# Stage one of a Fourier transform by float32r products of split sums, and a back stage given out later

## The chip, the cores and the metric

The kernel runs on one core of a Trainium2 chip. The metric is the device time of one execution in microseconds. Five engines work side by side, each through its own instructions in order: PE (matrix products, with a weight load before each, "PEld"), DVE, ACT and POOL (elementwise work) and SP (here only transfers). They wait for each other through semaphores.

## The reference

```python
def _attn_ref(x, w_r, w_i, b_r, b_i):            # x: 8 x 3008 x 256
    X = np.fft.rfft(x, axis=1)
    Yr = Xr @ w_r - Xi @ w_i + b_r
    Yi = Xr @ w_i + Xi @ w_r + b_i
    ...                                          # both shrunk: sign(Y) * max(|Y| - 0.01, 0)
    return np.fft.irfft(Y, n=3008, axis=1).astype(np.float32)

def _moe_ref(x, w_in, w_out):                    # x: 24064 x 256, w_in: 256 x 2048
    r = np.maximum(x @ w_in, 0.0)
    return ((r * r) @ w_out).astype(np.float32)
```

The output of the first is the input of the second.

## The kernel before, in words

**The transform.** 3008 is 64 x 47. The forward transform of a batch is done in two stages. Stage one (class `Fwd`, and `Fwd2` for the second batch) works on 13 units of 120 rows: two rows of the input are added and subtracted (`fold`, POOL, line 214, tile `xs`), and each of sum and difference is multiplied by a 120x120 matrix of cosines or sines (`am32`, line 235) in float32. The result is copied by ACT to `xe` and stored to DRAM (line 224). Stage two (class `Pair`) works on 12 pairs of groups in a batch: it loads stage one's result (`ka`), multiplies (line 279), mixes with the weights (line 300), shrinks, and goes back by the inverse matrix (`back`, line 332); `store_back` stores the result split in two (`kuh`, `kul`). `Back` loads that (`du`) and does the last transform (lines 455 to 459), whose output `yr` is the input of the second part.

**Products of split numbers.** Most products are done in float32r, a shorter format of the same four bytes. A float32 number is split into a high part and the rest, `hi` by a cast on ACT (line 97) and `lo` by a subtraction on POOL or DVE (line 101; both in `halves`), and a product is the sum of three: hi x hi, lo x hi, hi x lo. Stage one is done in plain float32; in the profile each float32 product shows as two records.

**The second part.** The tokens of a batch are six tiles of 500 or 504. For each tile there are eight steps of 21 float32r products with `win` (7 sums by a scheme of Strassen's kind; tile `psh`) and 12 with `wout` (`pso`). Between them stand DVE (sums, `mc`), ACT (relu, square, and the cast to `mg`'s high part) and POOL (`mg`'s low part). The input of a tile is split into `yt` in four pieces (`Tokens.split`); the last piece is needed by the second product of the tile's first step, and POOL writes its low part.

**The order.** The main loop runs over half steps, 96 in a batch. In each it issues half of a step and the jobs due by then: a job has a due time in half steps, for a pair `start + j * step` with fixed distances (`fwd` at 0, `sums` at 1.0, `mix` at 2.1 and 3.0, `shrink` at 4.0, `back(0)` at `end`, `back(1)` 0.9 later), for a unit of stage one its load 2.5 before, its fold 0.8 before and its product 0.3 after its time. While batch b is in the second part, the pairs of b + 1 and stage one of b + 2 are done. These are priorities: a scheduler lays the final order of each engine at build time from its own estimate of the times, and the engines then follow that order. Within the second part the order of the products is fixed (`then`). `T` takes a buffer of a named pool; the number of buffers of a name is in `MAIN` (2 if it isn't listed).

## Time and profile before

| | |
|---|---|
| median of 3 runs | 2624.49 us (2619.64 to 2627.85) |
| the profiled execution | 2624.28 us, its span 2622.5 us |
| busy, share of the span | PE 98%, DVE 68%, ACT 64%, POOL 63% |
| stage one by float32 (line 235) | 312 records of 379 ns, 199.4 to 2030.3 us |
| fold (line 214) | 156 instructions, 750 ns each |
| mean granted clock of TensorE | 0.992 |

A row of the timeline gives the start in microseconds, the duration, the engine, the line, the operation, what is written and read, and how many equal instructions it stands for; in brackets how long the engine had been idle before it and for whom. Rows of the waits give the total, the number and the longest in microseconds. Products overlap on PE, so a single record is longer than the distance from one to the next.

### The profile page before, as it was taken

To read this page: it belongs to the slowest core of one execution; us is meant where nothing else is said; L and a number is where in the kernel's file an instruction comes from. 1 tells how busy PE (TensorE), PEld (TensorE's weight loads), DVE (VectorE), ACT (ScalarE), POOL (GpSimd) and SP (SyncE) were. 2 spreads that over 40 slices of the span, in tenths; PEclk is the share of its full clock that TensorE was granted. 3 is DMA by queue.
4 is the path that set the end of the run, shared out by engine and by line. 5 is a ranking of instruction groups with operands and counts; after the bars stand their busy time and mean duration, and the time that the engine had idled before them with its cause. 6 is when DMAs were issued, how large, how long until landed. Compare 5 with 4: busy or idle time off the path is not lost.

```text
span 2622.5 us, 47568 instructions
## 1 busy us (share of the span) xinstructions
PE 2568.5 (98%) x16908; PEld 2348.8 (90%) x16908; DVE 1779.7 (68%) x3797; ACT 1671.7 (64%) x2433; POOL 1654.6 (63%) x1628
## 2 busy tenths in 40 slices
PE   6799999999999999999999999999999999999999
PEld 4688989999999999999999999999999999999998
DVE  6866766676666767577675776767767677765554
ACT  3466656666666666666666666666666666666665
POOL 3246656766676667667675676666666666666564
PEclk8899999999999999999999999999999999999999
DMA  8643333233422333223332333323332223221100
GB/s 269 195 140 98 113 108 89 83 108 92 117 85 81 108 105 96 85 86 110 107 95 85 96 99 107 94 75 104 99 104 88 72 81 95 76 66 38 36 17 17
DMA packets 191455, 250.51 MB, mean 96 GB/s; under 512 B 21755, under 2 KB 135923, under 8 KB 191219
## 3 DMA queue, kind: packets, MB, share of 16 engines
q1 hardware_dynamic: 178915, 225.12, 28.3%
q0 software_dynamic: 12304, 22.35, 3.7%
q8 instruction: 136, 2.23, 0.4%
q14 instruction: 100, 0.82, 0.1%
HBM read 146.85 MB, written 100.53 MB: 94 GB/s over the span
## 4 chain that ended last, share of the span: by engine, by line
PE 91%; DVE 3%; DMA 2%; POOL 2%; issue 1%; ACT 1%; SPq 0%; POOLq 0%; ACTq 0%; DVEq 0%
PE pso L478 38%; PE psh L478 34%; PE psf L300 7%; PE psf L279 3%; PE psf L235 2%; PE psf L332 2%; PE psf L458 1%; PE psf L459 1%; PE psf L455 1%; DMA s<-xe 1%; POOL mg L101 1%; DMA du<-s 1%; PE psf L409 1%; DMA x<-x_in 0%; DVE df L151 0%
## 5 line engine op out<-in xcount | busy, mean ns | idle before, releaser
L101 POOL TENSOR_TENSOR mg<-mc,mg 128x500 fp32r<-128x500 f32 (+1 forms) x768 | 973.6, 1288 | 587.5 <-ACT mg L97 557.7
L478 PE MATMUL pso<-mg,wout 128*128 128x500 f32 (+1 forms) x4608 | 1180.6, 393 | 3.9 <-POOL mg L101 2.6
L478 PE MATMUL psh<-yt,win 128*128 128x250 f32 (+1 forms) x8064 | 1070.1, 281 | 1.4 <-POOL yt L101 1.4
L478 ACT ACTIVATE mc<-mc 128x1000 f32<-128x1000 f32 (+1 forms) x768 | 802.4, 1045 | 411.5 <-DVE mc L478 402.5
L478 PEld LDWEIGHTS psh<-yt,win 128*128 128x128 f32 x8064 | 1020.6, 189 | 33.7 <-POOL yt L101 1.6
L478 PEld LDWEIGHTS pso<-mg,wout 128*128 128x128 f32 x4608 | 819.4, 189 | 132.7 <-POOL mg L101 4.8
L478 DVE TENSOR_TENSOR mc<-psh,mv 128x500 f32<-128x500 f32 (+3 forms) x768 | 419.4, 548 | 433.8 <-PE psh L478 401.8
L97 ACT CAST mg<-mc 128x1000 fp32r<-128x1000 f32 (+1 forms) x384 | 396.9, 1034 | 18.6 <-ACT mc L478 0.7
L478 DVE TENSOR_TENSOR mv<-psh,mu 128x500 f32<-128x500 f32 (+1 forms) x384 | 260.8, 679 | 55.6 <-PE psh L478 24.2
L300 PE MATMUL psf<-wx,kxh 128*128 128x256 f32 x1008 | 207.8, 282 | 1.4 <-ACT kxh L97 0.9
L98 DVE COPY mp<-psh 128x250 f32<-128x250 f32 (+1 forms) x384 | 160.0, 417 | 35.3 <-PE psh L478 11.5
L300 PEld LDWEIGHTS psf<-wx,kxh 128*128 128x128 f32 x1008 | 167.2, 189 | 5.9 <-ACT kxh L97 1.1
L101 POOL TENSOR_TENSOR ksl<-kv,ksh 128x512 fp32r<-128x512 f32 x84 | 108.6, 1293 | 95.8 <-ACT ksh L97 95.6
L478 DVE TENSOR_TENSOR mu<-psh,mp 128x250 f32<-128x250 f32 (+1 forms) x384 | 160.7, 419 | 11.5
L214 POOL TENSOR_TENSOR xs<-xt 120x256 f32<-120x256 f32 x156 | 114.0, 750 | 85.0 <-DMA xt<-x_in 77.3
L478 DVE TENSOR_TENSOR mc<-psh,mp 128x250 f32<-128x250 f32 (+1 forms) x384 | 157.1, 409 | 4.7 <-PE psh L478 3.1
L321 DVE TENSOR_TENSOR kv<-psf,ke 64x256 f32<-64x256 f32 x336 | 141.8, 422 | 22.4 <-PE psf L300 13.7
L300 PE MATMUL psf<-wx,kxl 128*128 128x256 f32 x504 | 141.5, 281 | 0.9 <-DVE kxl L101 0.9
L97 ACT COPY dy<-psf 128x188 f32<-128x188 f32 x256 | 76.6, 313 | 88.0 <-PE psf L459 87.8
L97 ACT CAST ksh<-kv 128x512 fp32r<-128x512 f32 x84 | 52.0, 619 | 118.4 <-DVE kv L101 112.7
L312 DVE TENSOR_TENSOR ke<-psf,bias 128x512 f32<-128x512 f32 x84 | 58.1, 691 | 100.2 <-PE psf L300 100.0
L97 ACT CAST kuh<-psf 128x256 fp32r<-128x256 f32 x192 | 68.5, 373 | 85.9 <-PE psf L332 67.4
(97 smaller groups left out, 2563.6 us busy)
## 6 DMA issues: line engine op xcount, KB each, us to landing
du<-s SPq DMA_DIRECT2D x128, 256.0 KB, 2.9
s<-kuh SPq DMA_DIRECT2D x192, 128.0 KB, 1.8
s<-kul SPq DMA_DIRECT2D x192, 128.0 KB, 1.9
s<-xe SPq DMA_DIRECT2D x92, 240.0 KB, 2.4
xt<-x_in SPq DMA_DIRECT2D x91, 240.0 KB, 3.5
kcm<-cm_in POOLq DMA_DIRECT2D x84, 256.0 KB, 3.3
ka<-s SPq DMA_DIRECT2D x84, 256.0 KB, 3.5
du<-s SPq DMA_DIRECT2D x256, 64.0 KB, 2.7
```

The source lines that it names most:

```text
L97: return act.copy(out=out, in_=in_)
L98: return eng.tensor_copy(out=out, in_=in_)
L101: return eng.tensor_tensor(out=out, in0=a, in1=b, op=ALU.subtract)
L214: return eng.tensor_tensor(out=out[:, :n], in0=self.xt[:, :n, 0], in1=self.xt[:, :n, 1], op=(ALU.add, ALU.subtract)[t])
L235: nc.tensor.matmul(ps[:M1, t], am32[:, t], self.u[:, t], start=True, stop=True)
L279: nc.tensor.matmul(pv[:, :, c, g, :], self.a[:, g, c * 128:(c + 1) * 128], bg, start=True, stop=True)
L300: self.last = nc.tensor.matmul(ps, l, wx[j][:, k, c, :], start=n == 0, stop=n == 5)
L312: dve.tensor_add(out=self.e, in0=self.pe, in1=bias)
L321: dve.tensor_add(out=v[64 * r:64 * r + 64, g], in0=ps[gs], in1=self.e[gs, r])
L332: nc.tensor.matmul(ps[:, :D], self.cm[:, g, j * 128:(j + 1) * 128], r[:, g], start=n == 0, stop=n == 2)
L409: nc.tensor.matmul(ps[:, :D], self.x[:, c, js], w32[j][:, c], start=n == 0, stop=n == 3)
L478: last_of[eng] = op(*args, **kwargs)
```

## The change

Stage one of the six last batches (class `Fwd`, 78 units) is done in float32r. After the fold the sums `xs` are split into `xh` (ACT) and `xl` (POOL), which share the two buffers of `xt`; the matrices are split once into `amh` and `aml`, the latter in the buffer of `nam`, after its last reader. Each of a unit's two float32 products becomes three. `Fwd2`, the second batch, stays as it was. And `end`, the due time of a pair's back stage, goes from 7.1 to 9.1 for the pairs of all but the first batch of the main loop, where it was 9.1 already. Line numbers behind the class `Fwd` grow by three (235 is 238, 279 is 282, 300 is 303, 332 is 335, 478 is 481).

```diff
@@ class Fwd
         def add(self):
-            self.u = T("xs", [M1, 2, D], F32)
+            u = T("xs", [M1, 2, D], F32)
             for t in range(2):
-                self.fold(pool, self.u[:, t:t + 1], t)
+                self.fold(pool, u[:, t:t + 1], t)
+            self.uh = T("xh", [M1, 2, D], F32R, tag="xt")
+            self.ul = T("xl", [M1, 2, D], F32R, tag="xt")
+            halves(self.uh, self.ul, u, pool)

         def run(self):
             ps = bank([128, 2, D])
             for t in range(2):
-                nc.tensor.matmul(ps[:M1, t], am32[:, t], self.u[:, t], start=True, stop=True)
+                for n, (a, u) in enumerate(((amh, self.uh), (aml, self.uh), (amh, self.ul))):
+                    nc.tensor.matmul(ps[:M1, t], a[:, t], u[:, t], start=n == 0, stop=n == 2)
...
-    nam = T("nam", [M1, M1], F32)
-    act.mul(nam, am32[:, 1], -1.0)
+    nam = T("nam", [M1, 2, M1], F32)
+    act.mul(nam[:, 0], am32[:, 1], -1.0)
...
-                first, step, end = 1.0, 6.1, 7.1
+                first, step, end = 1.0, 6.1, 9.1
...
         if m == max(LATER):
             conv.close()
             pools.update(dict.fromkeys(CONV), **dict.fromkeys(SIDE, memory(ctx, "side")))
+            amh, aml = (T(name, [M1, 2, M1], F32R, tag=tag) for name, tag in (("amh", "amh"), ("aml", "nam")))
+            halves(amh, aml, am32, pool)
```

With the jobs the scheduler's order changes. Three places of it follow; a name ends in the number of its buffer, and `x2` stands for two rows alike.

The first is PE at the start of the third tile (`yt_2391` and `yt_2392`, in the change `yt_2411` and `yt_2412`, are its high and low parts). Before, from the tile's first product:

```order
L478 MATMUL psh_2683<-yt_2391,win_81 128x250
L478 MATMUL psh_2683<-yt_2391,win_82 128x250
L478 MATMUL psh_2683<-yt_2392,win_81 128x250
L332 MATMUL psf<-ksh,kcm 128x256 x2
L332 MATMUL psf<-ksl,kcm 128x256
L235 MATMUL psf<-xs,am_76 120x256 x2
L279 MATMUL psf<-kb,ka 128x2x64 x4
```

Then come the three products that read the last piece. In the change:

```order
L481 MATMUL psh_2715<-yt_2411,win_81 128x250
L335 MATMUL psf<-ksh,kcm 128x256 x2
L335 MATMUL psf<-ksl,kcm 128x256
L481 MATMUL psh_2715<-yt_2411,win_82 128x250
L481 MATMUL psh_2715<-yt_2412,win_81 128x250
L238 MATMUL psf<-xh,amh 120x256
L238 MATMUL psf<-xh,aml 120x256
L238 MATMUL psf<-xl,amh 120x256
```

The same three of L238 follow for the difference, then the four of L282, and then thirteen products of L303 and six of L335, which are new here, before the one that reads the low part of the last piece.

The second is POOL up to the third tile's last split. Before:

```order
L101 TENSOR_TENSOR yt_2392<-yr,yt_2391 128x500
L494 TENSOR_TENSOR ms<-yr,ms 128x250
L101 TENSOR_TENSOR mg_2558<-mc,mg_2557 128x504 x2
L101 TENSOR_TENSOR yt_2392<-ms,yt_2391 128x500
L101 TENSOR_TENSOR ms<-yr,ms 128x250
L108 DMA kcm<-cm_in 128x512
L471 COPY yr<-dy 128x2x184
L101 TENSOR_TENSOR yt_2392<-ms,yt_2391 128x500
L101 TENSOR_TENSOR ksl<-kv,ksh 128x512
L214 TENSOR_TENSOR xs<-xt 120x256 x2
L101 TENSOR_TENSOR mg_2643<-mc,mg_2642 128x504 x2
```

In the change:

```order
L101 TENSOR_TENSOR yt_2412<-yr,yt_2411 128x500
L101 TENSOR_TENSOR mg_2586<-mc,mg_2585 128x504 x2
L497 TENSOR_TENSOR ms<-yr,ms 128x250
L101 TENSOR_TENSOR yt_2412<-ms,yt_2411 128x500
L108 DMA kcm<-cm_in 128x512
L101 TENSOR_TENSOR ms<-yr,ms 128x250
L474 COPY yr<-dy 128x2x184
L101 TENSOR_TENSOR ksl<-kv,ksh 128x512
L101 TENSOR_TENSOR mg_2671<-mc,mg_2670 128x504 x2
L214 TENSOR_TENSOR xs<-xt 120x256 x2
L101 TENSOR_TENSOR yt_2412<-ms,yt_2411 128x500
```

The last split (the last row with `yt`) went behind ksl, the next mg and the next xs. An xl stands above these rows.

The third is POOL up to the fifth tile's last split. Before:

```order
L101 TENSOR_TENSOR yt_3926<-yr,yt_3925 128x500
L214 TENSOR_TENSOR xs<-xt 120x256 x2
L494 TENSOR_TENSOR ms<-yr,ms 128x250
L101 TENSOR_TENSOR yt_3926<-ms,yt_3925 128x500
L101 TENSOR_TENSOR mg_4177<-mc,mg_4176 128x500 x2
L108 DMA kcm<-cm_in 128x512
L101 TENSOR_TENSOR ms<-yr,ms 128x250
L101 TENSOR_TENSOR ksl<-kv,ksh 128x512
L101 TENSOR_TENSOR kxl<-kp,kxh 128x256
L471 COPY yr<-dy 128x2x124
L101 TENSOR_TENSOR yt_3926<-ms,yt_3925 128x500
```

In the change:

```order
L101 TENSOR_TENSOR yt_3994<-yr,yt_3993 128x500
L101 TENSOR_TENSOR yt_3994<-ms,yt_3993 128x500
L101 TENSOR_TENSOR ms<-yr,ms 128x250
L214 TENSOR_TENSOR xs<-xt 120x256 x2
L101 TENSOR_TENSOR mg_4141<-mc,mg_4140 128x500 x2
L474 COPY yr<-dy 128x2x124
L101 TENSOR_TENSOR yt_3994<-ms,yt_3993 128x500
```

Before, `mg_4177` was the 32nd step's; in the change `mg_4141` is the 31st step's. The split went ahead of the 32nd, and a kcm, a ksl and a kxl went from above it to below.

6 lines of the change are left out of this document (3 added, 3 removed).

## The prediction

> **What bounds the kernel now.** I read the page's busy shares and its chain of waits first, then the busy time of each engine by stretches of the span.
>
> ```profile
> PE 2568.5 (98%) x16908; PEld 2348.8 (90%) x16908; DVE 1779.7 (68%) x3797; ACT 1671.7 (64%) x2433; POOL 1654.6 (63%) x1628
> PE 91%; DVE 3%; DMA 2%; POOL 2%; issue 1%; ACT 1%; SPq 0%; POOLq 0%; ACTq 0%; DVEq 0%
> 300.00:500.00 200.00, 193.93 (x1267) 177.03 (x1266) 132.03 (x276) 122.36 (x179) 124.75 (x126) 0.97 0.35 100
> 500.00:800.00 300.00, 299.98 (x2018) 276.43 (x2018) 204.52 (x441) 195.99 (x285) 203.86 (x204) 1.00 0.33 96
> 1700.00:2000.00 300.00, 299.76 (x2020) 276.38 (x2019) 207.71 (x443) 195.56 (x286) 203.97 (x204) 1.00 0.33 96
> ```
>
> The columns of the last three rows are PE, PEld, DVE, ACT and POOL busy, then granted clock, DMA share and GB/s. From 500 us on PE is never without a matmul (299.98 and 299.76 of 300), at full clock, and the chain that ends last is PE for 91%. There PE work taken away is time taken away, for as long as the helpers keep delivering. They have room: POOL is busy 203.86 of 300 (68%), ACT 195.99 (65%). The exception is the first batch. Between 200 and 500 us PE loses time at two places, and both matter for the change:
>
> ```profile
> 240.00:262.00 22.00, 19.31 (x125) 17.26 (x124) 13.95 (x29) 11.44 (x19) 17.45 (x19) 1.00 0.37 107
> 350.00:384.00 34.00, 27.96 (x163) 24.68 (x162) 19.04 (x41) 16.54 (x31) 22.06 (x25) 0.85 0.45 123
> ```
>
> The first loses 22.00 - 19.31 = 2.7 us, at full clock. The second is idle 34.00 - 27.96 = 6.0 us and has a mean clock of 0.85, which costs another 0.15 x 34 = 5.1 us: 11.1 us in all. Together 13.8 us.
>
> **Stage one on PE.** A unit's two float32 products (L235) give way to six float32r products of the same 256 columns. Both prices stand side by side in the trace, with a stream of float32r products (L300, six for each of two mixes) right before a unit of stage one:
>
> ```profile
> L235 PE MATMUL psf<-xs,am 120*120 120x256 f32 x312 | 81.2, 379 | 1.3 <-DVE kv L321 1.3
> 1018.65 0.28 PE L300 MATMUL psf<-wx,kxh 128*128 128x256 f32 x1
> ...
> 1020.06 1.03 PE L235 MATMUL psf<-xs,am 120*120 120x256 f32 x4
> 1008.10 2.60 PE L478 MATMUL psh<-yt,win 128*128 128x250 f32 x21
> ```
>
> The 312 records are 78 units of four, two records to a float32 product. A row that merges several records lasts one full record plus the starts in between, so records start every (1.03 - 0.379) / 3 = 0.217 us, and a unit holds PE for 4 x 0.217 = 0.868 us. The twelve float32r products start from 1018.65 to 1020.06: 1.41 / 12 = 0.1175 us each. Six cost 0.705 us. A unit saves 0.163 us, 78 units 12.7 us. The trace has no float32r product of 120 rows. The nearest row on the cheap side is the 250-column stream, (2.60 - 0.281) / 20 = 0.116 us, where 0.281 is the 0.28 us of one record as in the L300 row: 0.172 us a unit, 13.4 us. On the dear side, the saving is gone only at 0.868 / 6 = 0.145 us a product, a quarter above any stream shown. I take 12.7, since L300 has the very width.
>
> The Trainium skill ("FP8 and Floating Point Precision", TensorE Precision Notes) says that true FP32 takes four passes through the array. By that rule three passes instead of four would save a quarter of 0.868, an estimate of 16.9 us in all; the trace agrees on four passes only roughly, since a float32r product costs 0.1175 us and not the 0.1085 us of half a record.
>
> **The added split.** Each unit gains an ACT cast and a POOL subtraction of 120x512. The rows of the nearest shape, 128x512, and POOL's waits for xt, of which the rivals speak:
>
> ```profile
> L101 POOL TENSOR_TENSOR ksl<-kv,ksh 128x512 fp32r<-128x512 f32 x84 | 108.6, 1293 | 95.8 <-ACT ksh L97 95.6
> L97 ACT CAST ksh<-kv 128x512 fp32r<-128x512 f32 x84 | 52.0, 619 | 118.4 <-DVE kv L101 112.7 <-PE psf L332 5.5
> ```
>
> ```profile
> POOL xs L214 <- DMA xt<-x_in: 77.3, 44, 6.5
> ```
>
> 78 x 1.293 = 100.9 us more on POOL, 78 x 0.619 = 48.3 us more on ACT. With 13 units in a batch of 96 half steps this raises POOL from 68% to about 73%. In steady state it is hidden by POOL's idle time. What it costs if that cover is gone shows at a tile boundary, where POOL is busiest:
>
> ```profile
> 686.59 2.49 POOL L101 TENSOR_TENSOR mg<-mc,mg 128x500 fp32r<-128x500 f32 x2
> 689.04 1.07 POOL L101 TENSOR_TENSOR yt<-ms,yt 128x500 fp32r<-128x500 f32 x1
> 691.10 0.69 PE L478 MATMUL pso<-mg,wout 128*128 128x500 f32 x2
> 693.22 2.60 PE L478 MATMUL psh<-yt,win 128*128 128x250 f32 x21
> ```
>
> The tile's last split (yt) ends at 690.1. Of the 21 products from 693.22, nine still belong to the tile before and three don't need this split, so it is wanted at 693.22 + 12 x 0.116 = 694.6: 4.5 us to spare. The first half of mg ends near 687.9 and is wanted at 691.1: 3.2 us to spare. One xl of 1.29 us ahead of them is covered, two (2.6 us) nearly use it up. The new order puts one ahead of this place, and I count 0.5 us for all such places, between 0 and 3.
>
> **The two places of the first batch.** At the third tile PE waits for the last split:
>
> ```profile
> 237.03 1.44 POOL L214 TENSOR_TENSOR xs<-xt 120x256 f32<-120x256 f32 x2 [2.79 <-DMA xt<-x_in]
> 246.69 1.10 PE L235 MATMUL psf<-xs,am 120*120 120x256 f32 x4 [1.28 <-DVE kv L321]
> 249.47 1.06 POOL L101 TENSOR_TENSOR yt<-ms,yt 128x500 fp32r<-128x500 f32 x1
> 247.63 1.06 PE L279 MATMUL psf<-kb,ka 128*128 128x128 f32 x8
> 250.58 1.08 PE L478 MATMUL psh<-yt,win 128*128 128x250 f32 x7 [1.42 <-POOL yt L101]
> 255.95 2.51 POOL L101 TENSOR_TENSOR mg<-mc,mg 128x504 fp32r<-128x504 f32 x2
> ```
>
> POOL works without a pause from 237.03 to 250.53. The new order puts four more things ahead of that split: xl (1.29), ksl (1.29), the next mg (2.51) and the next xs (1.44), 6.5 us, so the split ends near 257.1. PE for its part has most of a pair's mix and two more groups' back stages ahead of the product that needs it. Summed by the prices above, with 0.9 us for the eight records of L279, that product moves from 2.7 to 4.8 us behind the tile's first, so from 249.2 (250.58 - 1.42) to about 251. The wait grows from 1.4 to some 6 us; if the 1.28 us in front of L235 goes, the place loses 6.4 instead of 2.7: +3.7 us. Without the reordering of PE it would be +6.5.
>
> The fifth tile is the second place:
>
> ```profile
> 354.78 1.42 POOL L214 TENSOR_TENSOR xs<-xt 120x256 f32<-120x256 f32 x2 [2.49 <-DMA xt<-x_in]
> 357.45 3.50 PE L478 MATMUL pso<-mg,wout 128*128 128x500 f32 x8 [2.42 <-POOL mg L101]
> 374.71 1.07 POOL L101 TENSOR_TENSOR yt<-ms,yt 128x500 fp32r<-128x500 f32 x1
> ```
>
> ```profile
> 356.00:359.00 3.00, 1.55 (x4) 1.30 (x5) 0.41 (x2) 0.94 (x2) 3.00 (x4) 0.70 0.46 116
> 359.00:362.00 3.00, 3.00 (x17) 2.62 (x16) 0.31 (x1) 0.00 (x0) 3.00 (x4) 0.74 0.00 0
> 374.00:377.00 3.00, 3.00 (x16) 2.99 (x15) 1.05 (x2) 0.37 (x1) 1.78 (x3) 0.50 0.36 112
> ```
>
> POOL sat in front of an xs whose input had not landed, mg stood behind it, PE ran dry and then worked at a clock of 0.70, 0.74 and later 0.50. Counted along POOL's order, the last split of the fifth tile stood behind the mg of all 32 steps of the four tiles before it, so it could not start until the last of their products had gone through DVE, ACT and POOL. The last split of the third tile stood behind 15 of 16. The change turns this round: 16 of 16 at the third tile, 31 of 32 at the fifth. At a place one mg short the loss was 2.7 us, so the fifth tile would come down from 11.1 to 2.7. The transfer of xt may be as late as before, though, which leaves it at 11.1. I take the middle, 7.0, and so 4.1 us off, between 0 and 8.4.
>
> The clock adds a term to the third tile. A wait of 2.42 us was followed here by 0.70 and 0.74 over two stretches of 3 us, which cost 0.30 x 3 + 0.26 x 3 = 1.7 us. The 6 us of the third tile should do no less: +1.7, and 3.0 if its clock falls to 0.50 for 6 us.
>
> The Trainium skill ("TensorE: Matmul & The Clock Gate", What you observe and What's actually happening in Part 1) has a window of some 3.4 us: an idle one halves the clock, and a busy one gives it back. By that rule a 6 us wait always costs a slow window, an estimate of 0.5 x 3.4 = 1.7 us, the same as from the rows; the trace agrees that the clock falls, though after a wait shorter than the window and not at once to a half.
>
> **The later back stage.** From the second to the seventh batch of the main loop the back stage of a pair moves from 7.1 to 9.1 half steps behind its start. It moves two reads of ksl, kcm and four stores on SP; kcm (two buffers) is held as much longer, but the next load of that buffer comes 5.9 half steps after the new end. In the waits of before PE's only stop at these products is the first row below, 0.3 us, so there is nothing to gain. What could be lost is the end of a batch, where the first tile of the next batch is read back behind the last stores:
>
> ```profile
> PE psf L332 <- DVE kul L101: 0.3, 1, 0.3
> ```
>
> ```profile
> 741.91 0.89 SPq L254 DMA_DIRECT2D s<-kul  x2
> 744.39 1.46 SPq L108 DMA_DIRECT2D du<-s  x3
> 463.28 1.29 POOL L101 TENSOR_TENSOR yt<-ms,yt 128x504 fp32r<-128x504 f32 x1
> 483.73 0.52 PE L478 MATMUL psh<-yt,win 128*128 128x252 f32 x3
> ```
>
> The read (du) follows the last store by 1.6 us. But the first batch already ends its last back stage at 11.2 + 11 x 5.3 + 10.0 = 79.5 half steps, later than the new 1.0 + 11 x 6.1 + 10.0 = 78.1, and its next tile (the first with 252 columns) had its split done at 464.6, 19 us before use. Two half steps, some 6.4 us, fit into that. Term: 0; if the cover were gone, up to 6.4 us at each of six ends.
>
> **The sum.** Against the profiled execution's own 2624.28 us (span 2622.5, 1.8 around it): -12.7 + 3.7 + 1.7 - 4.1 + 0.5 + 0 = -10.9, so 2613.4 us. The runs' median, 2624.49, is 0.2 above that execution.
>
> **Rivals.** *Both first-batch losses shrink* (0.10): the third tile stays at 2.7 and the fifth comes down to it, 5.4 instead of 13.8, since they hang on when single transfers land. 2624.3 - 12.7 - 8.4 = 2603 us. Against it: the third tile's list on POOL is 6.5 us longer. *The first batch gets worse* (0.25): the fifth tile gives nothing back (4.1), the third tile draws 0.50 for 6 us, not 1.7 but 3.0, and its split comes another 2.5 us later because xs again finds its input not landed, as the row of 354.78 shows (2.49): 2613.4 + 4.1 + 1.3 + 2.5 = 2621 us, no change to be told. *ACT is held by the fold* (0.13), the slower case: the cast of xh stands in ACT's queue until POOL has done xs, and POOL stands in front of xs until xt has landed (77.3 us in 44 waits, up to 6.5). Relu, square and mg of the main chain now queue behind it on ACT, where before only POOL stood still. It decides once such a wait uses up the 3.2 us of mg. A wait of 6.5 us then leaves 3.3 us on PE; three such in each of four batches are 40 us, and the time would be 2624.3 - 12.7 + 40 = 2651 us. Against it: with those 44 waits PE stood still for 0.3 us in the 600 us of the two full rows at the top. The forecast itself has 0.52.
>
> **How the numbers follow.** 0.3%, 7.9 us, is about what this measurement can tell from no change. Faster (below 2616.6): the forecast's 0.52 but for 0.02, and 0.10 of the first rival, 0.60. Same: 0.25 and the 0.02, 0.27. Slower: 0.13. The forecast's own range is 2608 to 2618, mostly the fifth tile's 4.1 us up and 4.3 down, and about 1 us from the price of a product. To hold 8 in 10 I reach down to 2602 and up to 2626, which leaves the slower case out.
>
> **What would show it.** Right: 468 matmul records of stage one, starting 0.117 us apart; PE full from 500 us on; POOL near 73% and ACT near 67% there; PE waiting some 6 us at the third tile near 250 us, and less than 6 us in all at the fifth. Wrong: PE waits for mg or yt that recur in later batches, rows of ACT xh waiting for POOL xs for long, or stage one's products starting 0.14 us apart or more.

## The result, and the profile after

The changed kernel takes 2638.54 us (median of 4 runs, 2635.66 to 2640.52) where the kernel before takes 2624.24 beside it: a ratio of 1.0057, with a 95% interval of 1.0044 to 1.0069. It is 14.3 us slower; 2613.4 was forecast. The profiled execution took 2639.22 us, 14.9 more than that of before.

The page of the changed kernel, busy shares and chain of waits; and its busy time by stretches, first two places of the first batch, then the sum of six stretches of 300 us from 500 to 2300 us (PE, PEld, DVE, ACT, POOL busy; behind a single stretch the granted clock, DMA share, GB/s):

```profile
PE 2565.6 (97%) x17064; PEld 2350.0 (89%) x17064; DVE 1802.1 (68%) x3797; ACT 1703.4 (65%) x2512; POOL 1756.0 (67%) x1707
PE 87%; DVE 6%; DMA 3%; issue 2%; POOL 1%; ACT 1%; SPq 0%; POOLq 0%; ACTq 0%; DVEq 0%
```

```profile
240.00:275.00 35.00, 29.92 (x180) 27.19 (x180) 20.62 (x42) 18.46 (x32) 25.23 (x26) 0.85 0.31 87
350.00:384.00 34.00, 30.34 (x197) 28.08 (x197) 22.67 (x47) 20.36 (x32) 28.77 (x30) 0.90 0.40 116
...
sum 1800.00, PE 1786.30 PEld 1649.98 DVE 1264.44 ACT 1195.37 POOL 1276.20; mean PE 297.72 PEld 275.00 DVE 210.74 ACT 199.23 POOL 212.70
```

The kernel before, the same view:

```profile
240.00:275.00 35.00, 32.31 (x211) 29.14 (x210) 23.64 (x50) 21.40 (x35) 24.93 (x27) 1.00 0.41 120
...
sum 1800.00, PE 1799.53 PEld 1660.61 DVE 1248.15 ACT 1176.91 POOL 1206.44; mean PE 299.92 PEld 276.77 DVE 208.02 ACT 196.15 POOL 201.07
```

From 500 to 2300 us, where PE stood idle for 0.5 us in all, it now stands idle for 13.7. POOL has 70 us more to do there and is busy 71% (212.70 of 300), ACT 66%; 73% and 67% were forecast. What PE waits for is new. The rows are sums over the whole execution. From 500 to 2300 us kp and mu have all of theirs, mg 1.7 us, kxh and mc 1.5 us each; the longest wait for kxh, of 3.0 us, lies in the first batch.

```profile
PE psf L303 <- ACT kxh L97: 5.6, 4, 3.0
PE psf L303 <- DVE kp L293: 5.1, 5, 1.8
PE psh L481 <- DVE mc L481: 3.2, 4, 1.6
PE pso L481 <- POOL mg L101: 2.4, 7, 0.9
PE psh L481 <- DVE mu L481: 1.9, 2, 1.1
```

**Where the 14.9 us came from.** The DVE copy mp is made once in each of the 384 steps, right behind the step's first products:

```profile
L98 DVE COPY mp<-psh 128x250 f32<-128x250 f32 (+1 forms) x384 | 160.0, 417 | 47.4 <-PE psh L481 25.9
```

Its start in the changed kernel less its start before, as a mean over 16 steps, gives the time lost or won up to there:

```
steps        us later in the changed kernel
first step    1.7
  16 to  31  12.3   (third tile, where the first batch lost time)
  32 to  47   2.9   (fifth tile's loss smaller)
  48 to  63   3.9   (first steps of the second batch)
  96 to 111   5.3
 192 to 207  10.1
 288 to 303  14.8
 320 to 335  15.3
last step    15.3
```

The two places of the first batch nearly cancel. The loss grows through the five batches behind it, by some 2.3 us each, in which the products should have won 2.0 each (13 units of 0.155 us, below). The 1.7 us of the first step are no effect of the change: three kernels of the experiments that are the kernel before itself up to there are 0.5, 1.8 and 2.3 us behind it.

**One place of them.** Rows of the changed kernel in order of time, of four engines:

```profile
1268.93 4.25 DVE L326 TENSOR_SCALAR kc<-kv 128x512 f32<-128x512 f32 x1
1269.17 1.30 POOL L101 TENSOR_TENSOR xl<-xs,xh 120x512 fp32r<-120x512 f32 x1
1270.42 2.47 POOL L101 TENSOR_TENSOR mg<-mc,mg 128x500 fp32r<-128x500 f32 x2
1272.22 0.39 PE L481 MATMUL pso<-mg,wout 128*128 128x500 f32 x1
1273.83 0.41 DVE L293 TENSOR_TENSOR kp<-psf,kq 128x256 f32<-128x256 f32 x1
1274.27 0.41 ACT L97 CAST kxh<-kp 128x256 fp32r<-128x256 f32 x1 [5.27 <-DVE kp L293]
1274.38 0.36 PE L303 MATMUL psf<-wx,kxh 128*128 128x256 f32 x1 [1.77 <-DVE kp L293]
1274.81 0.75 POOL L101 TENSOR_TENSOR kxl<-kp,kxh 128x256 fp32r<-128x256 f32 x1 [1.92 <-issue]
```

kc, the clamp of the shrink, takes 0.42 us where nothing is in its way. Here it took 4.25: POOL worked without a pause from 1249 us until 1272.89, and kc ended 0.29 us after that. Behind it in DVE's queue stood kp, behind that ACT's kxh, and PE ran out of products. Between 480 and 2270 us eleven of 69 kc took more than 2.5 us, and each ended 0.29 us after the end of an unbroken run of POOL; before, there was one. Waits of PE that follow such a kc within 6 us of its end add up to 10.0 us, of 14.0 in that stretch.

Not every kc had to wait for the end of a run. In the same stretch 42 took over 0.5 us, and 24 of them ended 0.28 or 0.29 us behind an instruction of POOL that another followed at once. In 22 of these the follower was a subtraction, and it took some 0.18 us longer than such a one does elsewhere (1.45 us for a half of mg instead of 1.27): there DVE did get in between. What decides between the two was not found.

The Trainium skill ("SBUF — State Buffer", Who interferes with whom) says that a DVE instruction with two SBUF inputs, or in a two-port mode, and a GpSimd instruction exclude each other, the second one waiting until the first has ended. The trace agrees that they exclude each other, and 29 of the 42 clamps waited for one instruction of POOL alone; ahead of the other 13, the eleven longest among them, up to four ended.

### The profile page after: what moved, and what is told of

The parts are those of the page before. It is cut to its first block, busy times and chain, and to the rows that moved or that the text cites. A ratio compares the mean times of both kernels' runs of the same rounds, so it can differ in the third digit from the quotient of the medians.

```text
span 2637.5 us, 47985 instructions
## 1 busy us (share of the span) xinstructions
PE 2565.6 (97%) x17064; PEld 2350.0 (89%) x17064; DVE 1802.1 (68%) x3797; ACT 1703.4 (65%) x2512; POOL 1756.0 (67%) x1707
## 4 chain that ended last, share of the span: by engine, by line
PE 87%; DVE 6%; DMA 3%; issue 2%; POOL 1%; ACT 1%; SPq 0%; POOLq 0%; ACTq 0%; DVEq 0%
PE pso L481 37%; PE psh L481 33%; PE psf L303 7%; PE psf L282 2%; PE psf L335 2%; PE psf L238 2%; PE psf L462 1%; PE psf L461 1%; PE psf L458 1%; DMA s<-xe 1%; DVE kv L324 1%; DVE kc L326 1%; DMA s<-kuh 1%; DVE mc L481 1%; DMA x<-x_in 0%
## 5 line engine op out<-in xcount | busy, mean ns | idle before, releaser
L481 PE MATMUL pso<-mg,wout 128*128 128x500 f32 (+1 forms) x4608 | 1163.4, 391 | 3.8 <-POOL mg L101 2.4
L97 ACT CAST mg<-mc 128x1000 fp32r<-128x1000 f32 (+1 forms) x384 | 397.0, 1034 | 13.4 <-ACT mc L481 0.4
L303 PE MATMUL psf<-wx,kxh 128*128 128x256 f32 x1008 | 220.7, 285 | 12.1 <-ACT kxh L97 5.6
L303 PEld LDWEIGHTS psf<-wx,kxh 128*128 128x128 f32 x1008 | 171.8, 191 | 21.2 <-ACT kxh L97 6.9
L481 DVE TENSOR_TENSOR mu<-psh,mp 128x250 f32<-128x250 f32 (+1 forms) x384 | 160.2, 417 | 10.4
L303 PE MATMUL psf<-wx,kxl 128*128 128x256 f32 x504 | 143.4, 285 | 2.1 <-DVE kxl L101 2.0
L468 DVE TENSOR_TENSOR yr<-psf,dy 128x188 f32<-128x188 f32 (+4 forms) x256 | 78.6, 312 | 63.8 <-ACT dy L97 61.3
L101 POOL TENSOR_TENSOR yt<-yr,yt 128x250 fp32r<-128x250 f32 (+1 forms) x94 | 88.0, 938 | 49.5 <-ACT yt L97 49.5
```

Source lines behind the costliest of these rows:

```text
L97: return act.copy(out=out, in_=in_)
L101: return eng.tensor_tensor(out=out, in0=a, in1=b, op=ALU.subtract)
L303: self.last = nc.tensor.matmul(ps, l, wx[j][:, k, c, :], start=n == 0, stop=n == 5)
L468: dve.tensor_add(out=o, in0=ps[:, 0, lo:hi], in1=y[:, c, lo:hi])
L481: last_of[eng] = op(*args, **kwargs)
```

## The experiments

The theories: **A**, the subtraction xl makes POOL late, or its runs long, and PE waits for what stands behind; **B**, the later back stage, or the order that came with it, put products where PE has to wait; **C**, the slower rival of the prediction, ACT is held by the cast of xh. The diffs show the lines that matter, and `...` marks what is left out. In some kernels the order of every engine was laid first and single instructions were changed or added after that; the text says of them "in its own order".

### The two halves of the change

Split sums alone, the back stage left at 7.1:

```diff
-                first, step, end = 1.0, 6.1, 9.1
+                first, step, end = 1.0, 6.1, 7.1
```

> The change with the back stage left at 7.1 half steps, so stage one by split sums alone. Theory A (POOL's longer unbroken runs of work, made by the added subtraction, hold up DVE's clamp kc, and PE waits for DVE behind it): the waits of PE between 500 and 2300 us stay near the 13.7 us of the changed kernel, some kc still take over 3 us, and the time is 2633 to 2642 us. Theory B (the later back stage put the mixes where PE has to wait): those waits fall below 3 us, and the time is 2622 to 2630 us.

Measured: 2640.67 us, ratio 1.0071 (1.0054 to 1.0087), and 13.3 us idle on PE from 500 to 2300 us. The loss comes with the split. Its place moved: with the back stage at 7.1 PE stands before ksh, once in each batch, and again behind a held kc: 10.4 of its 13.7 us of waits between 480 and 2270 us follow a kc of over 2.5 us. Four of the five waits before ksh were followed by 3.4 us at a granted clock of 0.50, by estimate 4 x 1.7 = 6.8 us that no idle time shows. The row of POOL below is the last of its run; it ended at 1267.15, kc at 1267.44.

```profile
1262.59 4.85 DVE L326 TENSOR_SCALAR kc<-kv 128x512 f32<-128x512 f32 x1
1266.09 1.06 POOL L101 TENSOR_TENSOR yt<-ms,yt 128x500 fp32r<-128x500 f32 x1
1268.87 0.51 PE L335 MATMUL psf<-ksh,kcm 128*128 128x256 f32 x2 [2.13 <-ACT ksh L97]
```

The later back stage alone, on the kernel before:

```diff
-                first, step, end = 1.0, 6.1, 7.1
+                first, step, end = 1.0, 6.1, 9.1
```

> The kernel before with the back stage at 9.1 half steps, stage one in float32 as before. Theory A: PE's waits between 500 and 2300 us stay below 2 us, no kc takes more than 2.8 us, and the time is 2620 to 2628 us. Theory B: 8 us of waits or more in that stretch, 2632 us or more.

Measured: 2630.41 us, ratio 1.0022 (1.0012 to 1.0032). PE is idle for 0.1 us from 500 to 2300 us, as A has it, yet the kernel is 6.8 us slower, and that was expected by neither. In its profiled execution steps 56 to 312 took 6.3 us longer. Added up over the distances from one record to the next, 3.6 us of that lie behind products of the back stage and 3.6 behind the 252-column products, in pieces of 0.1 to 0.2 us that no row shows as idle; 1.8 us come back at the 504-column pso. What makes these pieces was not traced. On top of the split the same edit makes the time no longer (2640.67 and 2638.54, with overlapping intervals), so its price depends on what it stands beside.

### Load without products, products without load

The whole change, but the products in float32 from the unsplit sums:

```diff
-                for n, (a, u) in enumerate(((amh, self.uh), (aml, self.uh), (amh, self.ul))):
-                    nc.tensor.matmul(ps[:M1, t], a[:, t], u[:, t], start=n == 0, stop=n == 2)
+                nc.tensor.matmul(ps[:M1, t], am32[:, t], self.u[:, t], start=True, stop=True)
```

> The whole change with its split, but the products of stage one in float32 from the unsplit sums as before; xh and xl are made and read by nothing. It has the helpers' load and the later back stage without the six products. Theory A: waits as in the changed kernel, and 78 x 0.034 = 2.7 us less on PE: 2633 to 2639 us. If the six products, in two or three places apart, were what costs: at most 2628 us, and waits below 4 us.

Measured: 2644.18 us, ratio 1.0074 (1.0059 to 1.0089), 9.6 us idle on PE. The helpers' load costs without the products, and the products take time off on top of it: the kernel with them is 5.6 us faster. The time lies above both ranges: the expectation had the sign of the products wrong, by a reading that the next run settles.

The kernel before with three products each, and no split:

```diff
-            self.u = T("xs", [M1, 2, D], F32)
+            self.u = T("xs", [M1, 2, D], F32R)
...
-                nc.tensor.matmul(ps[:M1, t], am32[:, t], self.u[:, t], start=True, stop=True)
+                for n, a in enumerate((amh, aml, aml)):
+                    nc.tensor.matmul(ps[:M1, t], a[:, t], self.u[:, t], start=n == 0, stop=n == 2)
```

> The kernel before (back stage at 7.1) with three float32r products for each float32 product of stage one, but without the split of the sums: the fold writes float32r at once, and all three products read it (its low part is left out, the product with aml stands twice). No cast, no subtraction. By the distances from the start of a unit to the start of what follows it (0.676 us before, 0.710 after) the time is 78 x 0.034 = 2.7 us above the kernel before, 2624 to 2630 us, with waits below 2 us from 500 us on. By the prediction's price it would be 12.7 us below it, 2608 to 2614 us.

Measured: 2618.39 us, ratio 0.9983 (0.9973 to 0.9992), between the two expectations. The 2.7 us came from the distance between a unit's first record and the record behind it. That distance deceives in float32, as the rows of the kernel before show:

```profile
1020.06 1.03 PE L235 MATMUL psf<-xs,am 120*120 120x256 f32 x4
1020.74 0.80 PE L478 MATMUL pso<-mg,wout 128*128 128x500 f32 x2
1021.38 0.85 PE L478 MATMUL psh<-yt,win 128*128 128x250 f32 x6
```

The pso behind the unit starts 0.68 us after it, but these two pso take 0.80 us where two take 0.61 or 0.62 elsewhere: 0.19 us of the float32 unit fall on the record behind it. 0.68 + 0.19 = 0.87, and over 61 such units the median is 0.867. In the changed kernel a unit takes 0.712, with nothing left over:

```profile
1008.25 0.28 PE L238 MATMUL psf<-xh,amh 120*120 120x256 f32 x1
...
1008.84 0.28 PE L238 MATMUL psf<-xl,amh 120*120 120x256 f32 x1
1008.96 0.40 PE L335 MATMUL psf<-ksh,kcm 128*128 128x256 f32 x2
```

So the products save 78 x 0.155 = 12.1 us of PE, and 12.7 was predicted. Of the 12.1 some 5 us arrive in the time (2623.24 to 2618.39), though POOL and ACT have nothing more to do here; PE is idle 2.9 us more from 500 to 2300 us, and the rest was not followed.

A larger lever at the same place, two products instead of three:

```diff
-                for n, a in enumerate((amh, aml, aml)):
+                for n, a in enumerate((amh, aml)):
```

> The kernel before with two float32r products (amh and aml with the sums, which the fold writes as float32r) for each float32 product of stage one; the low part of the sums is left out, and there is no cast or subtraction. A unit takes 4 x 0.1185 = 0.474 us of PE where it took 0.867, read over the unit and the record behind it: 0.393 x 78 = 30.7 us. If all of it arrives: 2589 to 2597 us. If it arrives as the 12.1 us of the run with three products did (4.9, two fifths), because the helpers come later against PE: 2608 to 2614 us.

Measured: 2600.21 us, ratio 0.9911 (0.9896 to 0.9926). 23 of 30.7 us arrive, between the two expectations. It is the fastest kernel of this study, 0.9% below the kernel before, at the price of the sums' low part: they are rounded to float32r.

### POOL's load, with every order kept

The changed kernel in its own order, with a shorter xl. After the order is laid, each instruction passes through this; in the second of the two kernels 64 is 256, and the product reads `[1, 256]`:

```diff
...
+    if "TensorTensor" in kind and i.outs[0].memref.startswith("xl"):
+        ins, outs = ([copy.replace(a, ap=[a.ap[0], [1, 64]]) for a in side] for side in (i.ins, i.outs))
+        return copy.replace(i, ins=ins, outs=outs)
+    if "Matm" in kind and any(a.memref.startswith("xl") for a in i.ins):
+        ins = [
+            copy.replace(a, ap=[a.ap[0], [0, 4], [1, 64]], offset=0) if a.memref.startswith("xl") else a for a in i.ins
+        ]
+        return copy.replace(i, ins=ins)
...
```

> The changed kernel with every engine's order left as it is, but the subtraction that makes xl works on 64 of its 512 columns (the rest of the low part is left out: the product that reads xl takes these 64 columns four times over). POOL has some 1.0 us a unit less to do, and nothing else is moved. Theory A (POOL's added work is the cause): PE's waits between 500 and 2300 us fall from 13.7 to below 4 us, no kc takes over 3 us, 2625 to 2631 us. Rival (the order itself, or the products in pieces between others): at least 10 us of waits stay, 2635 us or more.

> The changed kernel in its own order, with xl made of 256 of its 512 columns (the rest of the low part is left out; both products read the same 256). POOL's work for a unit lies between the 0.33 us of the run with 64 columns (2618.25 us) and the 1.30 us of the change (2638.54 us), near 0.73. If every microsecond of POOL's work costs alike, 2618.25 + 20.3 x (0.73 - 0.33) / (1.30 - 0.33) = 2626.6 us, 2624 to 2630. If there is an edge behind which POOL's runs of work grow together: within 3 us of one of the two ends.

Measured: 2618.25 us with 64 columns, ratio 0.998 (0.9971 to 0.9989), and 2622.80 with 256, ratio 1.000 (0.9991 to 1.001). POOL's row of xl in each, 64 columns first; then the sum of the six stretches with 64 columns:

```profile
L101 POOL TENSOR_TENSOR xl<-xs,xh x78: 312/326/775, 198.6 to 2020.9; 120x64 fp32r<-120x64 f32 x78
...
sum 1800.00, PE 1797.46 PEld 1662.47 DVE 1257.20 ACT 1204.29 POOL 1227.94; mean PE 299.58 PEld 277.08 DVE 209.53 ACT 200.71 POOL 204.66
```

```profile
L101 POOL TENSOR_TENSOR xl<-xs,xh x78: 727/744/1186, 197.8 to 2025.5; 120x256 fp32r<-120x256 f32 x78
```

With the order, the products, the cast of xh and the back stage all as in the change, and only xl cut from 1.30 to 0.33 us, 20.3 us are gone and the idle time of PE falls from 13.7 to 2.5 us. That is theory A, which gave 2625 us at the least, and it leaves B and C no more than a small part. The run with 256 columns met neither of its expectations (2624 to 2630 us, or within 3 us of one of the ends). It is no straight line: from 0.33 to 0.74 us a microsecond of POOL costs 4.55 / (78 x 0.418) = 0.14 us, from 0.74 to 1.30 it costs 15.7 / (78 x 0.556) = 0.36. Drawn on to an xl of nothing by the first of these, the change would stand at 2618.25 - 0.14 x 78 x 0.33 = 2614.7 us.

By the starts of mp the kernel with 64 columns is 4.1 us earlier than before at steps 48 to 63, and 5.9 at steps 320 to 335. So it wins 1.8 us there, where the products of 65 units should win 10.1: some 8 us still go from the second batch on. To see whether these are the later back stage, the same with the back stage at 7.1:

```diff
-                first, step, end = 1.0, 6.1, 9.1
+                first, step, end = 1.0, 6.1, 7.1
```

> The split sums with the back stage at 7.1 half steps, and xl made of 64 of its 512 columns after the order is laid (the rest of the low part is left out). If the 8 us that the run with 64 columns and the later back stage (2618.25 us) still loses from the second batch on are those of the later back stage, this kernel takes 2609 to 2614 us. If they are what is left of the split (the cast, 0.33 us of POOL, the order): 2616 us or more.

Measured: 2622.61 us, ratio 0.9995 (0.9985 to 1.0004), 7.2 us idle on PE. They are not: beside the split the earlier back stage is dearer, as in the run of the split alone. Where the 8 us go stays open. One candidate is what is left of the split: the cast, the 0.33 us of POOL, the order that came with them, and the two buffers of xt that xh and xl share. Another needs no split: the kernel with three products and no split is 4.7 us earlier than before at steps 48 to 63 and 9.0 at steps 320 to 335, so it wins 4.3 us where 10.1 were due, and 5.8 us go there too.

The other way round: the kernel before in its own order, with a subtraction behind each of the 78 pairs of folds, whose result nothing reads (a and b are the tiles `bias` and `spare`; it waits for POOL's own earlier instructions alone):

```diff
...
+        if "TensorTensor" in type(i).__name__ and i.outs[0].memref.startswith("xs"):
+            n += 1
+            if n % 2 == 0:
+                out.append(copy.replace(
+                    i, name=f"I-9{n:08d}", ins=a + a, outs=b,
+                    sync_info=mybir.SyncInfo(on_wait=[copy.replace(wait, wait_value=before)], on_update=[]),
+                ))
...
```

> The kernel before with every engine's order as it was, and behind each of the 78 folds one more subtraction of 120x512 on POOL, whose result nothing reads. It adds the 1.29 us a unit of xl to POOL and nothing else. Theory A: PE waits 5 us or more between 500 and 2300 us, some kc take 3 us or more, 2629 to 2642 us. Rival (POOL at 73% has the room, as the prediction held; the order of the change or the products cost): waits below 2 us there, 2620 to 2628 us.

Measured: 2641.78 us, ratio 1.0071 (1.0056 to 1.0086), 9.7 us idle on PE. The added instruction took 1.04 us, 81 us in all, and made the kernel 18.5 us slower without a product, a cast or an order changed. The order of PE is the same as before, so record can be compared with record: between 480 and 2270 us 13.6 us come in, 6.6 in front of pso, which reads mg, and 6.2 in front of psh, which waits for DVE's mc. 9.6 of the 13.6 show as idle; a record of PE lasts some 0.16 us longer than the distance to the next, and a wait within that doesn't show. PE's two rows of the whole execution, and the kernel's rows of a place that recurs in each batch:

```profile
PE pso L478 <- POOL mg L101: 8.4, 9, 3.8
PE psh L478 <- DVE mc L478: 4.5, 7, 1.6
...
1015.25 1.03 POOL L214 TENSOR_TENSOR spare<-bias 120x512 f32<-120x512 f32 x1
1015.81 3.19 DVE L323 TENSOR_SCALAR kc<-kv 128x512 f32<-128x512 f32 x1
1016.25 2.47 POOL L101 TENSOR_TENSOR mg<-mc,mg 128x500 fp32r<-128x500 f32 x2
1018.93 0.41 DVE L478 TENSOR_TENSOR mc<-psh,mv 128x250 f32<-128x250 f32 x1
```

### By which way: DVE held, or POOL late

Theory A has two ways. In A1 POOL's work holds up DVE, and PE waits for DVE; in A2 what POOL itself makes comes late. First the change with kv in PSUM, the memory into which PE writes its sums, instead of SBUF, where the other tiles lie; DVE's clamp and subtraction then have one operand in SBUF at most:

```diff
-                    dve.tensor_add(out=v[64 * r:64 * r + 64, g], in0=ps[gs], in1=self.e[gs, r])
+                    dve.tensor_add(out=pv[64 * r:64 * r + 64, 1 - g], in0=ps[gs], in1=self.e[gs, r])
...
-            dve.tensor_scalar(out=cl, in0=v, scalar1=-LAM, scalar2=LAM, op0=ALU.max, op1=ALU.min)
-            sub(dve, v, v, cl)
+            for g in range(2):
+                dve.tensor_scalar(out=cl[:, g], in0=pv[:, 1 - g], scalar1=-LAM, scalar2=LAM, op0=ALU.max, op1=ALU.min)
+            for g in range(2):
+                sub(dve, v[:, g], pv[:, 1 - g], cl[:, g])
```

> The whole change, with kv kept in the PSUM bank of the third mix until the clamp and the subtraction behind it have read it, each in two halves of 256 columns: DVE then has no instruction there whose operands all lie in SBUF. Theory A: no kc takes over 1 us, PE's waits between 500 and 2300 us fall from 13.7 to below 4, and the time is 2624 to 2632 us, the 2.7 us that the products of stage one cost and up to 5 us for a bank that is held longer. Theory C (ACT is held by the fold, through the cast of xh) and theory B: the waits stay, 2635 us or more.

Measured: 2649.62 us, ratio 1.0097 (1.0082 to 1.0112). The clamp, now twice 84 instructions of half the width, took 0.43 us at the most, with POOL nearly as busy as in the change (70%), so DVE is no longer held:

```profile
L329 DVE TENSOR_SCALAR kc<-psf 128x256 f32<-128x256 f32 x168 | 62.9, 416 | 0.9
```

But PE idles 17.4 us, and the time is what B and C gave: with the bank held longer, PE waits at other places. Taken alone the run decides nothing, so the kernel before got the same edit, with the back stage at 7.1 and at 9.1.

> The kernel before with kv in the bank of the third mix, as in the run of the change with it (2649.6 us). It gives the price of the longer-held bank alone. Theory A1 (POOL's work costs through DVE's instructions that it holds up; without them the change would be worth what its products save): the price is high, and this kernel takes 2648 to 2662 us, as much as the change with kv there or more. Theory A2 (POOL itself is late with mg and yt, and the holding of kc adds little): the change costs here what it costs elsewhere, so this kernel takes 2632 to 2640 us.

> The kernel before with the back stage at 9.1 half steps and kv in PSUM; beside the whole change with kv in PSUM (2649.6 us) it differs by the split sums and their products alone. Theory A1: without instructions of DVE that POOL holds up, the split is worth its products, so this kernel is slower than 2649.6 us by 4 to 14 us: 2653 to 2664 us. Theory A2: the split costs here what it costs elsewhere (2638.5 against 2630.4 us, 8 us): 2638 to 2645 us.

Measured: 2667.22 us (1.0166, 1.0151 to 1.0181) and 2663.09 us (1.0152, 1.0135 to 1.0169). The first lies above both of its ranges, the second in that of A1. Beside the second one, which differs from the change with kv in PSUM by the split and its products alone, the change is 13.5 us faster, about what the products save (12.1). So where DVE isn't held, the split costs nothing to be seen. These kernels have waits of their own, though (22.4 us idle in the second), in which a late POOL can hide as well, so what that says of the kernels without the edit is limited.

xl on DVE instead of POOL:

```diff
-            halves(self.uh, self.ul, u, pool)
+            halves(self.uh, self.ul, u, dve)
```

> The whole change with xl made on DVE. Theory A: POOL has no more to do than before, so PE's waits between 500 and 2300 us fall below 8 us and the time is 2626 to 2636 us; what is left would be xl itself, held on DVE like kc. Theory C (the cast of xh behind the fold holds ACT): waits as in the changed kernel, 2636 us or more.

Measured: 2645.68 us, ratio 1.0081 (1.0066 to 1.0096), 13.5 us idle on PE. POOL had no more to do than before, and it helped nothing. The time is in the range of C, but the runs with a shorter xl, in which the cast stays, speak against C. xl itself was now held, with all of DVE's work behind it: 0.68 us at the least, 1.09 in the median, 6.1 at the most. That this is what costs was not shown; the largest sum of PE's waits there from 500 to 2300 us, 3.9 us, is for loads of du.

```profile
L101 DVE TENSOR_TENSOR xl<-xs,xh x78: 680/1092/6095, 198.5 to 2044.1; 120x512 fp32r<-120x512 f32 x78
```

Last, POOL late without holding DVE. The kernel before in its own order, with a pause of POOL behind each pair of folds; the first of the three makes it of 40 register moves, the others of 50 and 16 waits for an event that has come:

```diff
...
+                for _ in range(50):
+                    k += 1
+                    out.append(copy.replace(event, name=f"I-9{k:08d}", sync_info=done))
...
```

> The kernel before in its own order; behind each of the 78 second folds POOL waits for that fold's end and then runs 40 register moves, in which it reads and writes no tile. mg and yt come later by this pause, as with the added subtraction, but DVE isn't held by it. If the pause is near 1 us: theory A1: kc at most 2.8 us, waits of PE below 4 us between 500 and 2300 us, 2622 to 2631 us. Theory A2: as with the added subtraction, 8 us of waits or more, 2635 to 2646 us.

> The kernel before in its own order; behind each of the 78 second folds POOL waits 50 times for that fold's end, which has come after the first, so it stands still for about 1 us (40 register moves made 0.24) and touches no tile in it. The added subtraction of 1.04 us at the same places made the time 18.5 us longer, with kc up to 4.7 us and 9.6 us of waits on PE between 480 and 2270 us. Theory A1 (DVE is held while POOL works): kc stays at 2.8 us at most, waits below 4 us, 2623 to 2632 us. Theory A2 (POOL's results come later): waits of 8 us or more, mostly for mg and yt, 2636 to 2646 us.

> As the run with 50 waits behind each of the 78 second folds, but with 16, which by its 3.22 us for 50 make POOL stand still for 1.03 us, as long as the added subtraction took (1.04 us, 18.5 us on the time). Theory A1 (DVE is held while POOL works): kc at most 3.1 us, waits of PE below 4 us between 480 and 2270 us, 2623 to 2632 us. Theory A2 (POOL's results come later): 8 us of waits or more, mostly for mg, 2636 to 2646 us.

Measured, with the pause read from the rows (the median over 78, of the time from the end of the fold to the next start, less that of the kernel before):

```
                     pause or work    in all     time above before    ratio (95%)
register moves           0.24 us       19 us         2.0 us           1.0010 (1.0001 to 1.0019)
added subtraction        1.04          81           18.5              1.0071 (1.0056 to 1.0086)
16 waits                 1.15          90           17.9              1.0061 (1.0044 to 1.0078)
50 waits                 3.22         251          127.6              1.0485 (1.0469 to 1.0500)
```

The first pause was too short and the second too long for what they were meant to tell. The third is the one, and it went against A1: a POOL that stands still, and lets DVE through (the longest kc is 2.77 us), costs as much as one that works. A2 has the time right and PE waits for mg, if with 7.0 us between 480 and 2270 us, of which 6.9 are for mg, and not the 8 that A2 gave at the least. Record compared with record 10.7 us come in there, all of them in front of pso. PE's row of the whole execution:

```profile
PE pso L478 <- POOL mg L101: 11.1, 17, 3.1
```

The same place in the kernel before and with the pause:

```profile
672.41 1.83 POOL L214 TENSOR_TENSOR xs<-xt 120x256 f32<-120x256 f32 x2 [4.83 <-DMA xt<-x_in]
674.20 2.50 POOL L101 TENSOR_TENSOR mg<-mc,mg 128x500 fp32r<-128x500 f32 x2
674.53 2.60 PE L478 MATMUL pso<-mg,wout 128*128 128x500 f32 x10
```

```profile
677.44 1.88 POOL L214 TENSOR_TENSOR xs<-xt 120x256 f32<-120x256 f32 x2 [4.79 <-DMA xt<-x_in]
679.60 1.07 PE L478 MATMUL pso<-mg,wout 128*128 128x500 f32 x4
680.43 2.48 POOL L101 TENSOR_TENSOR mg<-mc,mg 128x500 fp32r<-128x500 f32 x2 [1.12 <-ACT dy L97]
681.74 1.61 PE L478 MATMUL pso<-mg,wout 128*128 128x500 f32 x6 [1.06 <-POOL mg L101]
```

Before, POOL stands 4.83 us in front of the fold until xt has landed, does the fold, then mg. The first of the two mg ends at 674.20 + 1.25 = 675.45; the fifth of the ten pso is the first to read it, and starts at 674.53 + 4 x 0.227 = 675.44. There is nothing to spare. A pause of 1.1 us there is a wait of 1.06 us on PE.

So the way depends on the order and on what POOL does. In the order of before a pause costs through mg, which comes late, directly; a subtraction of the same length costs half that way and half through DVE. In the order of the change 10.0 us of PE's visible waits follow a held kc and few are for mg; of the 13.4 us between the short xl and the whole one, 8.0 stand in front of the products with kxh and 4.5 in front of psh. That the held kc is the way there rests on these rows, as the run that frees DVE has waits of its own. The amount, 18 to 20 us for 76 to 90 us of POOL, is the same in both.

## Why the prediction was wrong

- **The products** (-12.7): right as work of PE, 12.1 us by the records, 0.867 to 0.712 us a unit. Both prices, 0.868 and 0.705, were read as they are; the doubt of them in some of the expectations was the mistake, as the run with the products alone shows. As time they are not all there: "PE work taken away is time taken away, for as long as the helpers keep delivering", and with the products alone 4.9 of the 12.1 us arrive. What takes the rest was not followed.
- **"In steady state it is hidden by POOL's idle time"**, with 0.5 us for all places between 0 and 3: this is the step that failed. Cutting xl from 1.30 to 0.33 us took 20.3 us off the change, and 1.04 us of work behind each fold put 18.5 on the kernel before. The working took the time to spare from one place, a tile boundary, where POOL seemed busiest (4.5 us for the split, 3.2 for mg). Counted through the order for all 272 steps from 48 to 319, the first product that reads mg's low part starts less than 1 us behind it in 22 of them, less than 0.1 us in 4 (the 28th step of a batch, in four of the five), with 3.25 in the median. The tightest place stands not where POOL is busy but behind its longest wait for xt (4.83 us in the rows above). The term had to be a sum over such places through five batches, not one place's remainder.
- **What stood in the way of seeing it**: the waits of before were taken as the proof of room ("with those 44 waits PE stood still for 0.3 us in the 600 us"). A place at which mg ends in the very moment it is wanted shows no wait either. The busy share of POOL, 68 and then 71%, said nothing on it.
- **DVE** had no part in the prediction. That 1.29 us more on POOL makes a kc of 4.25 us on DVE could have been asked: before already had a kc of 2.57 us that ended 0.29 us behind POOL.
- **The third tile** (+3.7 and +1.7): from 240 to 275 us PE lost 35 - 29.92 = 5.1 us idle and 0.15 x 35 = 5.2 us of clock, 10.3 us against 2.7 before, so +7.6 where 5.4 was said. The way was another. PE did not wait for the last split but for kxh. Ahead of kxh in ACT's queue stood ksh, which waited 0.66 us for a kc and a kv - kc that POOL held; for the rest of the 3.04 us ACT was at work, on mc, ksh, kq and kxh itself:

```profile
249.72 1.36 DVE L326 TENSOR_SCALAR kc<-kv 128x512 f32<-128x512 f32 x1
251.12 1.48 DVE L101 TENSOR_TENSOR kv<-kv,kc 128x512 f32<-128x512 f32 x1
252.63 0.62 ACT L97 CAST ksh<-kv 128x512 fp32r<-128x512 f32 x1 [0.66 <-DVE kv L101]
254.06 0.58 PE L303 MATMUL psf<-wx,kxh 128*128 128x256 f32 x1 [3.04 <-ACT kxh L97]
258.85 1.07 POOL L101 TENSOR_TENSOR yt<-ms,yt 128x500 fp32r<-128x500 f32 x1
260.35 1.69 PE L481 MATMUL psh<-yt,win 128*128 128x250 f32 x7
```

  The split ended at 259.92 where 257.1 was said, in time for products that the first wait had put off. The clock had been misread, too. The 0.70 and 0.74 from which 1.7 us was taken are means over 3 us: cut at other times, the kernel before shows 1.00 from 354.0 to 357.1 us, 0.50 from 357.2 to 360.5 and 1.00 from 360.6 to 363.0, so the clock did fall at once to a half. One such stretch costs the 1.7 us, but here the half lasted 10.2 us, from 253.7 to 263.9, and cost 5.1:

```profile
252.00:255.00 3.00, 0.74 (x2) 0.45 (x2) 1.50 (x3) 2.37 (x5) 2.15 (x3) 0.78 0.94 262
255.00:258.00 3.00, 3.00 (x15) 3.00 (x16) 0.53 (x2) 0.75 (x2) 2.99 (x3) 0.50 0.92 250
258.00:261.00 3.00, 2.44 (x11) 2.07 (x11) 0.71 (x3) 1.26 (x3) 2.75 (x5) 0.50 0.26 87
261.00:264.00 3.00, 3.00 (x11) 2.56 (x11) 2.26 (x5) 0.00 (x0) 1.72 (x2) 0.52 0.58 157
```

- **The fifth tile** (-4.1): right in size, by luck. From 350 to 384 us 34 - 30.34 = 3.7 us idle and 0.10 x 34 = 3.4 us of clock, 7.1 us, where 7.0 stood in the working, as the middle of two cases. Neither case came. The wait of 2.42 us for mg behind the late xt is gone, and the waits at L279 and L300 (in the change L282 and L303), of which the working says nothing, stayed: 2.9 us from 367 to 373 us before, 3.7 from 372 to 378 in the change.
- **The later back stage** (0): +6.8 us alone, nothing to be told on top of the split. Not the end of a batch, of which the prediction was afraid; see the run.
- **The rivals.** ACT held by the fold (2651) had the side right, and its first half, POOL in front of an xs whose input has not landed. It does not take the cast of xh: the same loss came without any cast. *The first batch gets worse* (2621) had the third tile's clock of 0.50 right, and a later split there, with a loss of 9.2 us where 7.6 came; but the fifth tile did give back its 4.0.
- **The sum over again**, with what was measured: 1.7 us already there at the first step, which is the scatter of single executions; -12.1 for the products; +3.6 for the two places of the first batch (7.6 - 4.0); xl in the batches behind it +13.2, from the growth of 11.4 us in the change and of -1.8 with the short xl; and the 8.3 that the short xl leaves there, which is a remainder and not explained. Together 14.7, where the profiled executions are 14.9 apart.

## What to carry to other kernels

An engine that is idle a third of the time can still have no time to spare at the one place that recurs; count, for every repeat, how long before its first reader a result is ready, and look also behind the waits for a transfer, where an engine starts late. In this kernel work for POOL was also a load on DVE, where DVE's operands lie in SBUF, and moving xl from the one to the other did not get round that. Time saved on the fullest engine need not arrive in full: here 4.9 of 12.1 us did, and 23 of 30.7. To price a load alone, keep the order and change the length of one instruction, or add a pause; to price a stream of products, take the time to the record after next.

## What was not expected of the hardware

- DVE's clamp could be passed over by several instructions of POOL that follow each other at once. In eleven cases it took 2.6 to 4.3 us and ended 0.29 us after the end of an unbroken run; in 24 shorter ones it got in between two instructions.
- With one of the two operands in PSUM, or the only one, the same clamp and subtraction were never held (0.43 us at the most, over 168 of each).
- A float32 unit of four records leaves 0.19 us on the record behind it. A float32r unit leaves none.
- The granted clock fell to 0.50 at 253.7 us, in a wait of 3.04 us that followed one of 1.28, and stayed there until 263.9, though PE was idle for only 0.6 us of the 9 us from 255 on. From 500 to 2300 us single waits of up to 1.77 us left it at 1.00. In the run with the split alone waits of 1.89, 2.05, 2.07 and 2.09 us each brought 3.4 us at 0.50, and one of 2.13 us did not.
